# Reordering the first batch of an attention and mixer kernel: indices spread by a product, masks ahead of the data, casts on ScalarE

## The chip, the cores and the metric

The kernel runs on one core of a Trainium2 chip. The core has a matrix engine (TensorE, PE in the profile, with its weight loads as PEld), VectorE (DVE), ScalarE (ACT), GpSimd (POOL) and SyncE (SP), and 16 DMA engines that move data between memory and the core's SBUF. The engines run their own instruction lists in order and wait for each other by semaphores. The metric is the device time of one execution in microseconds, as the median of several runs.

## The reference

Eight batches with eight heads, 576 tokens and 64 elements a head. Attention is limited to a window of 32 tokens to either side, and eight tokens with given indices are global: they see all tokens, and all tokens see them. A token mixer and a channel mixer follow.

```python
scores = scale * np.matmul(q, k.transpose(0, 1, 3, 2))
mask = np.abs(pos[:, None] - pos[None, :]) <= window
mask = mask | is_global[:, None] | is_global[None, :]
attn = softmax(np.where(mask, scores, -1e9))        # written out in full
x = (attn @ v) with the heads side by side          # (8, 576, 512)
u = x + (np.maximum(x^T @ w_tok1, 0) @ w_tok2)^T
out = u + np.maximum(u @ w_ch1, 0) @ w_ch2
```

The indices are an input, so all masks that depend on them are made on the chip. The products run in float16, while inputs and the output are float32.

## The kernel before

The order of the instructions of each engine is the order in which the program is written: there is no planner, and an engine that waits holds back all that is written behind it. Two pools of PSUM tiles are used in turn: psS with three of them (scores, turned tiles, PV) and psM with two (the dense products).

A batch is worked on as follows. Heads are taken in four pairs p. `cast_qk` brings q and k to float16 (`qk`), and the last 64 of the 576 tokens of q and k together into `rn`. `T` turns a pair with products against an identity, `TE` copies the turned q and k from PSUM to `qT` and `kT`, including the last tokens. `S_` forms the scores of a pair in two parts and ACT takes the exponential into `e_all`. `SM` multiplies with the mask `bandm` on DVE. `GK` makes the rows of the global tokens (`lf`, masked by `mf`), `OG` their outputs (`rf`), and `PV` the product with v for each of five token tiles, with the division on DVE. `M1`, `M2` (for batch 0 `M23_first`) are the token mixer, `M3` turns its result, and `M4` and `M5` are the channel mixer, whose products are the list `dense`; `period(b)` spreads the dense products of batch b between the attention steps of batch b+1.

What comes ahead of `period(0)` is written out by hand at the end of the function (L781 to L860). There, the loads of q, k and v of batch 0 are issued from SP, pair by pair. Two loads from ACT's queue bring the indices: `gpp_i`, one index for each partition, and `gidx_b`, all eight for every partition (L78, L79). POOL writes constants and zero pads, makes `mf` in `masks_c` (L302, L303), clears the left part of `e_all` (L784), casts v in `castv`, issues the loads of the token mixer's weights (`load_wt`), the gathers of the global tokens' q and k of batches 0 to 3 (`gather(0)`, four indirect DMAs with the indices `idx_i`) and the loads of the channel mixer's first weights (`load_wc1`). Between the steps of the first pairs DVE makes the index masks: `masks_0` the one-hot tables for the global tokens of batch 0, `masks_a` the masks of rows and columns (with five products into `pcol`), `masks_b` their product with the band. `G0` picks the global tokens of batch 0 out of `qk` with a product. `gather_t(0)` stands between `PV(0,1)` and `PV(0,2)`: it casts what was gathered on ACT, turns it on PE and copies it.

In the first batch cast0(p) casts q on ACT and k on DVE. SP loads q and k of batch 1 into the same buffers as soon as these casts are done, ACT casts them after `GK(0)`, and `T(1,0)` and `T(1,1)` follow between the `PV` of batch 0.

Of the kernel before, what the change touches and what calls it, by code (L numbers as in the profile page):

```python
# [26 lines left out]
def kernel(  # L27
# [48 lines left out]
    gidx_b = const.tile([P, NG, 2], I32)  # L76
    gpp_i = const.tile([P, 1], I32)
    nc.scalar.dma_start(out=gpp_i, in_=bass.AP(tensor=gt32, offset=0, ap=[[0, P // NG], [2, NG], [1, 1]]))  # L78
    nc.scalar.dma_start(out=gidx_b.rearrange("p g w -> p (g w)"), in_=bass.AP(tensor=gt32, offset=0, ap=[[0, P], [1, 2 * NG]]))  # L79
# [32 lines left out]

    pi_i = const.tile([P, 1], I32)
# [26 lines left out]

    qk_pads(0)
# [30 lines left out]
    kgz = const.tile([P, B, NP, 2 * GW], F16)  # L172
    nc.vector.memset(kgz, 0.0)
    gpp = to_f("gpp", gpp_i, [P, 1])
    idx_i = const.tile([P, 4], I32)
    nc.vector.tensor_scalar(out=idx_i, in0=bc_f, scalar1=hb, scalar2=gpp, op0=ALU.add, op1=ALU.add)

    gpm = const.tile([P, 1], F32)
    nc.vector.tensor_scalar(out=gpm, in0=hi8, scalar1=-10000.0, scalar2=gpp, op0=ALU.mult, op1=ALU.add)
# [48 lines left out]
    e_all = const.tile([P, H, NT, EW], F16)  # L228
# [9 lines left out]

    def e_pads():
        nc.gpsimd.memset(e_all[:, :, 0, 64:P], 0.0)  # L240
        nc.gpsimd.memset(e_all[:, :, NT - 1, 64 + GW + P :], 0.0)

# [14 lines left out]

    def masks_0():
        nc.vector.tensor_copy(out=gidx_f, in_=gidx_b[:, :, 0])
        onehot(ohq, op_f, NT + 1)  # L260

    def masks_a():

        oht = const.tile([P, NT, NG], F32)
        isg = const.tile([P, NT], F32)
        onehot(oht, tp_f)
        nc.vector.reduce_sum(out=isg, in_=oht, axis=AX.X)
        isgb = const.tile([P, NT, P], F16)
        nc.vector.tensor_copy(out=isgb, in_=isg.unsqueeze(2).to_broadcast([P, NT, P]))
        pcol = [psm([P, 512], name="pcol0"), psm([P, P], name="pcol1")]  # L270
        for t in range(NT):
            nc.tensor.matmul(
                pcol[t // 4][:, P * (t % 4) : P * (t % 4) + P], lhsT=isgb[:, t, :], rhs=ident, start=True, stop=True
            )
# [9 lines left out]
        nc.vector.tensor_scalar(out=colng[:, 0:512], in0=pcol[0], scalar1=0.5, scalar2=None, op0=ALU.is_lt)  # L284
        nc.vector.tensor_scalar(out=colng[:, 512:S], in0=pcol[1][:, 0:LAST], scalar1=0.5, scalar2=None, op0=ALU.is_lt)
        nc.vector.memset(colng[:, S:], 0.0)

    def masks_b():
        rowh = const.tile([P, NT], F16)
        nc.vector.tensor_copy(out=rowh, in_=rowok)  # L290
        cn = colng.rearrange("p (c x) -> p c x", c=NT)
        bl, br = bandm[:, 1:NT, 0:64], bandm[:, :, 80:208]
        nc.vector.memset(bandm[:, 0, 0:64], 0.0)
        nc.vector.tensor_tensor(out=bl, in0=left.unsqueeze(1).to_broadcast([P, NT - 1, 64]), in1=cn[:, 0 : NT - 1, 64:P], op=ALU.mult)
        nc.vector.tensor_tensor(out=br, in0=right.unsqueeze(1).to_broadcast([P, NT, P]), in1=cn, op=ALU.mult)
        nc.vector.tensor_tensor(out=bl, in0=bl, in1=rowh[:, 1:NT].unsqueeze(2).to_broadcast([P, NT - 1, 64]), op=ALU.mult)
# [86 lines left out]
    def G0(p):  # L383

        if p == 0:
            st[0]["pg"] = psm([P, NP, 2, NG], name="pg0")
        pg = st[0]["pg"]
# [14 lines left out]
    def T(b, p):  # L402
        pT = pss([P, 2, 8 * P], F16, name=f"pT_{b}_{p}")
        for ti in range(2):
            for t in range(4):
                nc.tensor.transpose(out=pT[:, ti, P * t : P * t + P], in_=qk[:, ti, p, t], identity=ident)
        nc.tensor.transpose(out=pT[:, 1, 512:640], in_=rn[:, p], identity=ident)
        st[b]["pT", p] = pT

    def TE(b, p):  # L410
        pT = st[b]["pT", p]
        qT, kT = qTs[b % 2][:, p], kTs[b % 2][:, p]

        copy = nc.scalar.copy if b == 1 and p < 2 else nc.vector.tensor_copy
        pm = pT[:, 0, 0:512].rearrange("p (i t x) -> p t x i", i=4, t=4)
        copy(out=qT[:, 0:4, GW:QS].rearrange("p t (x i) -> p t x i", i=4), in_=pm)  # L416
        copy(out=qT[:, 4, GW : GW + LAST], in_=pT[:, 1, 512 : 512 + LAST])
        copy(  # L418
            out=kT[:, WIN : WIN + 512].rearrange("p (x i) -> p x i", i=4),
            in_=pT[:, 1, 0:512].rearrange("p (i x) -> p x i", i=4),  # L420
        )
        copy(out=kT[:, WIN + 512 : WIN + S], in_=pT[:, 1, 512 + LAST : 640])
# [168 lines left out]
    def M23_first(tau):  # L591
# [4 lines left out]
        for ch in range(2):  # L596
            nc.tensor.matmul(
                ps, lhsT=w2[:, ch, P * tau : P * tau + P], rhs=s["a1"][:, ch, :], start=(ch == 0), stop=(ch == 1)
            )
        nc.vector.tensor_add(out=s["u16"][:, tau], in0=x16s[0][:, tau], in1=ps)  # L600

    def M3_first(tau):
# [4 lines left out]
        nc.scalar.copy(out=s["uT"][:, :, P * tau : P * tau + P], in_=pu)  # L607
# [74 lines left out]
    def period(b):  # L682
# [12 lines left out]
        def scores(p, k):  # L695
# [12 lines left out]
            if n < 3 and p < 2:  # L708
                TE(n, p + 2)
# [53 lines left out]
        if n == 1:  # L763
            d(2)
            T(2, 0)
            TE(2, 0)
            T(2, 1)
            TE(2, 1)
# [7 lines left out]

    def cast0(p):
        cast_qk(0, 0, p, nc.scalar.copy)
        cast_qk(0, 1, p, nc.vector.tensor_copy)

    e_pads()  # L781
    pads(0)
    masks_c()
    nc.gpsimd.memset(e_all[:, :, :, 0:64], 0.0)  # L784
    castv(0)
    load_wt()
    gather(0)
    load_wc1(0)
    load_wc1(4)
    load_wc1(8)  # L790
    cast0(0)
    cast_qk(0, 0, None, nc.scalar.copy)
    masks_0()
    T(0, 0)
    cast0(1)
    TE(0, 0)
    G0(0)
    T(0, 1)
    cast0(2)
    TE(0, 1)  # L800
    es = S_(0, 0, 0)
# [91 lines left out]
```

## Time and profile before

| what | value |
|---|---|
| median of three runs | 329.54 us (328.32 to 329.64) |
| the profiled execution's own time | 328.06 us |
| its span | 326.0 us |
| busy PE, DVE, ACT, POOL | 296.4, 194.4, 163.8, 87.2 us |
| granted TensorE clock | 1.0 |

The span goes from the first to the last profiled instruction, and the profiled time has about two microseconds around it. A timeline row has the start, the length, the engine, the line, the operation, its output and inputs with their shapes, and in brackets how long the engine was idle before it and which work ended that. A row of groups has the number of instructions, their busy time together, the mean in ns of one, and the idle time ahead of them. The chain of work that ended last follows from the last instruction back to what released each. For a DMA, the profile gives the time from issue to landing.

### The profile page before, as it was taken

To read this page: it belongs to the slowest core of one execution; us is meant where nothing else is said; L and a number is where in the kernel's file an instruction comes from. 1 tells how busy PE (TensorE), PEld (TensorE's weight loads), DVE (VectorE), ACT (ScalarE), POOL (GpSimd) and SP (SyncE) were. 2 spreads that over 40 slices of the span, in tenths; PEclk is the share of its full clock that TensorE was granted. 3 is DMA by queue.
4 is the path that set the end of the run, shared out by engine and by line. 5 is a ranking of instruction groups with operands and counts; after the bars stand their busy time and mean duration, and the time that the engine had idled before them with its cause. 6 is when DMAs were issued, how large, how long until landed. Compare 5 with 4: busy or idle time off the path is not lost.

```text
span 326.0 us, 6430 instructions
## 1 busy us (share of the span) xinstructions
PE 296.4 (91%) x2541; PEld 155.6 (48%) x2541; DVE 194.4 (60%) x420; ACT 163.8 (50%) x296; POOL 87.2 (27%) x134
## 2 busy tenths in 40 slices
PE   1545989998999899999999999999999999999994
PEld 0333744544447444554457444644466445544641
DVE  4799558558774566767764557766773575360021
ACT  2439569411673846457645828385824455304600
POOL 8878957750593300230032000400000000000000
PEclk9999999999999999999999999999999999999999
DMA  5999999959379999794899289965530520043023
GB/s 137 267 263 165 203 178 272 180 155 275 103 180 214 153 223 318 112 90 110 262 234 114 50 238 294 124 66 144 125 56 13 148 68 2 0 87 125 0 72 92
DMA packets 107038, 48.18 MB, mean 148 GB/s; under 512 B 86336, under 2 KB 100544, under 8 KB 107008
## 3 DMA queue, kind: packets, MB, share of 16 engines
q1 hardware_dynamic: 67600, 32.52, 43.6%
q0 software_dynamic: 39120, 15.24, 38.8%
q8 instruction: 20, 0.33, 0.4%
q14 instruction: 10, 0.08, 0.1%
q10 hardware_dynamic: 288, 0.01, 0.0%
HBM read 36.12 MB, written 9.44 MB: 140 GB/s over the span
## 4 chain that ended last, share of the span: by engine, by line
PE 77%; DVE 13%; ACT 5%; DMA 2%; issue 1%; SPq 1%; DVEq 0%; ACTq 0%
PE op L653 28%; PE b1p L627 21%; PE a1p L556 5%; PE hp L580 4%; PE s L433 4%; PE b1lp L640 3%; DVE e_all L481 3%; PE pv L533 3%; PE pv L524 3%; PE pv L529 2%; ACT e_all L446 2%; DMA lk<-in_k_dram 2%; DVE qT L416 1%; ACT e_all L459 1%; ACT b L630 1%; DVE kT L418 1%
## 5 line engine op out<-in xcount | busy, mean ns | idle before, releaser
L627 PE MATMUL b1p<-uT,wc 128*128 128x512 f16 x384 | 94.8, 380 | 1.1 <-ACT b L630 0.3
L630 ACT ACTIVATE b<-b1p 128x512 f16<-128x512 f32 x96 | 58.4, 608 | 60.8 <-PE b1p L627 60.8
L653 PE MATMUL op<-wc,b 128*128 128x512 f16 x384 | 87.9, 379 | 0.0
L653 PEld LDWEIGHTS <-b 128*128 128x128 f16 x384 | 36.6, 98 | 43.8
L325 POOL DMA_DIRECT2D vsh<-in_v_dram x35 | 29.8, 867 | 96.4 <-PE pv L533 89.0
L627 PEld LDWEIGHTS <-wc 128*128 128x128 f16 x384 | 34.9, 98 | 43.3 <-issue 5.2
L446 ACT ACTIVATE e_all<-s 128x832 f16<-128x832 f32 x32 | 27.7, 866 | 52.9 <-issue 31.8
L657 DVE TENSOR_TENSOR osb<-u,op 128x512 f32<-128x512 f16 x32 | 22.0, 687 | 50.0 <-PE op L653 49.9
L481 DVE TENSOR_TENSOR e_all<-e_all,bandm 128x1040 f16<-128x1040 f16 x64 | 43.4, 718 | 1.2
L586 DVE TENSOR_TENSOR u<-x,hp 128x512 f16<-128x512 f16 x28 | 17.4, 683 | 21.6 <-PE hp L580 21.6
L541 DVE TENSOR_TENSOR x<-pv,rr 128x512 f16<-128x512 f32 (+1 forms) x40 | 27.6, 691 | 1.4
L524 PEld LDWEIGHTS <-e_all 128*128 128x128 f16 x320 | 22.0, 100 | 5.2 <-issue 0.2
L524 PE MATMUL pv<-vsh,e_all 128*128 128x66 f16 x320 | 24.3, 197 | 0.0
L433 PE MATMUL s<-qT,kT 64*128 64x208 f16 (+1 forms) x320 | 20.3, 254 | 4.2 <-DVE kT L418 1.8
L540 DVE RECIPROCAL rr<-pv 128x8 f32<-128x8 f32 (+1 forms) x40 | 8.3, 207 | 24.0 <-PE pv L533 23.8
L459 ACT ACTIVATE e_all<-s 128x576 f16<-128x576 f32 x32 | 20.9, 652 | 3.2 <-PE s L433 3.2
L529 PE MATMUL pv<-vsh,e_all 128*128 128x66 f16 x256 | 21.0, 198 | 0.0
L433 PEld LDWEIGHTS <-kT 64*128 64x128 f16 x320 | 12.0, 97 | 18.7 <-issue 12.6
L529 PEld LDWEIGHTS <-e_all 128*128 128x128 f16 x256 | 17.8, 101 | 3.4
L556 PE MATMUL a1p<-x,w 128*128 128x512 f16 x64 | 18.9, 379 | 0.0
L464 ACT ACTIVATE e_all<-s 128x416 f16<-128x416 f32 x32 | 17.1, 535 | 0.0
L533 PE MATMUL pv<-rf,lf 128*128 128x264 f16 x80 | 16.2, 285 | 0.9 <-DVE rf L508 0.9
(166 smaller groups left out, 343.5 us busy)
## 6 DMA issues: line engine op xcount, KB each, us to landing
out_dram<-osb SPq DMA_DIRECT2D x32, 256.0 KB, 3.2
lq<-in_q_dram SPq DMA_DIRECT2D x4, 1024.0 KB, 6.4
lk<-in_k_dram SPq DMA_DIRECT2D x4, 1024.0 KB, 8.9
wc<-in_moe_w_ch_dram POOLq DMA_DIRECT2D x6, 512.0 KB, 9.4
lq<-in_q_dram POOLq DMA_DIRECT2D x3, 1024.0 KB, 7.9
lk<-in_k_dram POOLq DMA_DIRECT2D x3, 1024.0 KB, 9.4
vsh<-in_v_dram POOLq DMA_DIRECT2D x21, 128.0 KB, 8.5
vsh<-in_v_dram POOLq DMA_DIRECT2D x14, 96.0 KB, 8.1
```

What stands on the lines that cost most here:

```text
L325: nc.gpsimd.dma_start(out=vsh[b % 2][r0:r1, c, :, 0:D], in_=v[b, :, j0 : j0 + (r1 - r0), :].rearrange("h p d -> p h d"),)
L433: nc.tensor.matmul(ps[:, par, off : off + n], lhsT=kT[r, P * c : P * c + P], rhs=qf[r, lo : lo + n], start=True, stop=True,)
L446: nc.scalar.activation(out=e2[:, :, 1:3, 64:EW], in_=ps[:, :, 0 : 2 * W].rearrange("p h (c x) -> p h c x", c=2), func=AF.Exp, scale=scale,)
L481: nc.vector.tensor_mul(out=eh, in0=eh, in1=bandm)
L524: nc.tensor.matmul(o, lhsT=e_all[:, h, tau, EW - P - sh : EW - sh], rhs=vsh[b % 2][:, tau, h, :], start=hh == 0, stop=False,)
L529: nc.tensor.matmul(o, lhsT=e_all[:, h, tau + 1, 0:P], rhs=vsh[b % 2][:, tau + 1, h, :], start=False, stop=False)
L533: nc.tensor.matmul(ps[:, hf, 0 : NP * VW], lhsT=s["lf"][:, P * tau - sh : P * tau - sh + P], rhs=s["rf"][:, 2 * hf : 2 * hf + 2], start=Fa ...
L541: nc.vector.tensor_tensor(out=x16s[b % 2][r, tau, :].rearrange("p (f h x) -> p f h x", f=2, h=NP), in0=pq[r, :, :, 0:D], in1=rr[r].unsquee ...
L556: nc.tensor.matmul(ps[tt], lhsT=w, rhs=x16s[b % 2][:, ch, :], start=(ch == 0), stop=(ch == NT - 1))
L627: nc.tensor.matmul(ps, lhsT=wc1[:, cc, P * j : P * j + P], rhs=s["uT"][:, cc, :], start=(cc == 0), stop=(cc == 3))
L630: nc.scalar.activation(out=s["b1"][:, j, :], in_=ps, func=AF.Relu)
L653: nc.tensor.matmul(ps, lhsT=w, rhs=wc2[:, j, :], start=(j == 0), stop=(j == NJ - 1))
```

## The change

The change is to the prologue, and to steps that the later batches share.

- The eight indices are loaded once, as one row in one partition (`gidx_1`), where two loads spread them over all partitions. `masks_0` casts the row and spreads it by a product with a row of ones into PSUM (`misc`). `positions()` works out `gpp`, `gpm` and `idx_i` on DVE from the spread indices and a selection table `sel`, and stands after the first scores.
- The zeros of `e_all` are written by DVE at the start, and no longer by POOL.
- `masks_0` and `masks_a` stand ahead of the casts of batch 0. The rest of the masks is split into `masks_b1`, `masks_b2` and `masks_b3`, which stand between the steps of the pairs.
- `cast0` puts q and k on ACT. In `TE` of the first two pairs q is copied by DVE and k by ACT, and the last tokens are turned for all four pairs in one step, `TR`, with two copies, in batches 0, 1 and 2.
- POOL's order becomes: pads, `load_wt`, `castv`, `masks_c`, `load_wc1(0)`, `gather(0)`, `load_wc1(4)`, `load_wc1(8)`.
- In `M23_first`, odd token tiles add x by a product with the identity and are copied by ACT; the last copy of `M3_first` is DVE's.
- `pcol`, `misc` and `pg` share two PSUM tiles that are taken once.

```diff
-    nc.scalar.dma_start(out=gpp_i, in_=bass.AP(tensor=gt32, offset=0, ap=[[0, P // NG], [2, NG], [1, 1]]))
-    nc.scalar.dma_start(out=gidx_b.rearrange("p g w -> p (g w)"), in_=bass.AP(tensor=gt32, offset=0, ap=[[0, P], [1, 2 * NG]]))
+    gidx_1 = const.tile([1, 2 * NG], I32)
+    nc.scalar.dma_start(out=gidx_1, in_=bass.AP(tensor=gt32, offset=0, ap=[[2 * NG, 1], [1, 2 * NG]]))
...
+    nc.vector.memset(ones, 1.0)
+    nc.vector.memset(e_all[:, :, :, 0:64], 0.0)
+    nc.vector.memset(e_all[:, :, 0, 64:P], 0.0)
+    nc.vector.memset(e_all[:, :, NT - 1, 64 + GW + P :], 0.0)
...
+    pm8 = int_op("pm8", 7, ALU.bitwise_and)
+    sel = to_f("sel", cc_i, [P, NG])
+    nc.vector.tensor_scalar(out=sel, in0=sel, scalar1=pm8, scalar2=None, op0=ALU.is_equal)
...
+    def positions():
+        nc.vector.tensor_mul(out=sel, in0=sel, in1=gidx_f)
+        nc.vector.reduce_sum(out=gpp, in_=sel, axis=AX.X)
+        nc.vector.tensor_scalar(out=gpm, in0=hi8, scalar1=-10000.0, scalar2=gpp, op0=ALU.mult, op1=ALU.add)
+        nc.vector.tensor_scalar(out=idx_i, in0=bc_f, scalar1=hb, scalar2=gpp, op0=ALU.add, op1=ALU.add)
...
     def masks_0():
-        nc.vector.tensor_copy(out=gidx_f, in_=gidx_b[:, :, 0])
+        gidx_h = const.tile([1, NG], F16)
+        nc.vector.tensor_copy(out=gidx_h, in_=gidx_1.rearrange("p (g w) -> p g w", w=2)[:, :, 0])
+        nc.tensor.matmul(misc[:, 0:NG], lhsT=ones, rhs=gidx_h, start=True, stop=True)
+        nc.vector.tensor_copy(out=gidx_f, in_=misc[:, 0:NG])
         onehot(ohq, op_f, NT + 1)
...
+    def TR(b, copy):
+        pr = pss([P, NP, P], F16, name=f"pr_{b}")
+        for p in range(NP):
+            nc.tensor.transpose(out=pr[:, p], in_=rn[:, p], identity=ident)
+        copy(out=qTs[b % 2][:, :, NT - 1, GW : GW + LAST], in_=pr[:, :, 0:LAST])
+        copy(out=kTs[b % 2][:, :, WIN + 512 : WIN + S], in_=pr[:, :, LAST:P])
...
+        if tau % 2 == 0:
+            nc.vector.tensor_add(out=s["u16"][:, tau], in0=x16s[0][:, tau], in1=ps)
+        else:
+            nc.tensor.matmul(ps, lhsT=ident, rhs=x16s[0][:, tau], start=False, stop=True)
+            nc.scalar.copy(out=s["u16"][:, tau], in_=ps)
...
+    qk_pads(0)
     pads(0)
-    masks_c()
-    nc.gpsimd.memset(e_all[:, :, :, 0:64], 0.0)
-    castv(0)
     load_wt()
+    castv(0)
+    nc.vector.memset(kgz, 0.0)
+    masks_0()
+    masks_a()
+    cast0(0)
+    T(0, 0)
+    cast_qk(0, 0, None, act)
+    TE_q(0, 0, dve)
+    TE_k(0, 0, act)
+    TR(0, dve)
+    G0(0)
+    cast0(1)
+    exps(S_(0, 0, 0))
+    T(0, 1)
+    positions()
+    masks_c()
+    load_wc1(0)
     gather(0)
-    load_wc1(0)
     load_wc1(4)
     load_wc1(8)
...
+    masks_b1()
+    TE_q(0, 1, dve)
     cast0(2)
+    exps(S_(0, 0, 1))
     G0(1)
+    TE_k(0, 1, act)
     T(0, 2)
+    masks_b2()
+    exps(S_(0, 1, 0))
+    TE(0, 2, dve)
     cast0(3)
+    exps(S_(0, 1, 1))
     G0(2)
     T(0, 3)
+    masks_b3()
+    exps(S_(0, 2, 0))
+    exps(S_(0, 2, 1))
+    SM(0, 0)
+    TE(0, 3, dve)
     G0(3)
     SM(0, 1)
+    exps(S_all(0, 3))
     GK(0)
+    SM(0, 2)
+    SM(0, 3)
     OG(0)
...
     gather_t(0)
+    TR(1, act)
```

125 lines of the change are left out of this document (47 added, 78 removed).

## The prediction

> **What bounds the kernel now.** I read the page first, then the chain in order of time, then the first 46 us engine by engine. The page gives the scale.
>
> ```profile
> span 326.0 us, 6430 instructions
> ...
> PE 296.4 (91%) x2541; PEld 155.6 (48%) x2541; DVE 194.4 (60%) x420; ACT 163.8 (50%) x296; POOL 87.2 (27%) x134
> ```
>
> PE bounds the whole, but not the start. The chain in order of time (start, length, what) is almost without a gap DVE's from 9.94 to the rf product, then goes over to PE, and from 46.12 on it is the b1p products of the regular periods.
>
> ```profile
> 9.94 0.57 DVE qk L336
> ...
> 31.57 0.72 DVE rf L508
> ...
> 46.12 0.97 PE b1p L627 x4
> ```
>
> So everything up to 46.1 us is prologue, and a microsecond won or lost there is carried to the end. The stretch from 9.94 to 32.28, by engine:
>
> ```profile
> 9.94:32.28 22.34, 12.44 (x146) 7.62 (x147) 21.43 (x58) 12.79 (x24) 18.47 (x23) 1.00 1.12 224
> ```
>
> The columns behind the length are busy PE, PEld, DVE, ACT, POOL, then PE clock, DMA share and GB/s. DVE is busy 21.43 of 22.34 us there; ACT has room; POOL has 18.47 us of work, which matters below.
>
> **The change, part by part.**
>
> DVE between 9.94 and 32.28 loses work. Its groups:
>
> ```profile
> L336 DVE CAST qk<-lk 128x512 f16<-128x512 f32 x3 | 3.6, 1210 | 2.3 <-DMA lk<-in_k_dram 2.3
> L418 DVE COPY kT<-pT 128x512 f16<-128x512 f16 x4 | 2.7, 678 | 0.0
> ...
> L481 DVE TENSOR_TENSOR e_all<-e_all,bandm 128x1040 f16<-128x1040 f16 x8 | 5.2, 696 | 0.2
> ...
> L422 DVE COPY kT<-pT 128x64 f16<-128x64 f16 x4 | 0.7, 178 | 0.0
> ...
> 17.72 0.19 DVE L253 TENSOR_TENSOR oht<-tp_f,gidx_f 128x40 f32<-128x40 f32 x1
> ...
> 20.03 0.68 DVE L284 TENSOR_SCALAR colng<-pcol 128x512 f16<-128x512 f32 x1
> ```
>
> A row of this view is count, busy us, mean ns, and idle time before; the last two rows are of the timeline (start, length). Gone: three k casts (3.6), two of four kT copies (1.36), and masks_a from 17.72 to 20.03 (2.3). The eight small last-token copies (L417 costs as L422, 1.4 together) become two larger ones, about 0.35 each by their size, between the 0.18 and 0.68 rows: saved 0.7. Added: positions(), four small operations of about 0.2 each, 0.8. Net 7.2 us less, so DVE has 14.2 us left. ACT, busy 12.79 us in this stretch, gets three casts at 0.62 (1.9) and two kT copies of about 0.68 (1.4): 16.1, so it has room, all the more as its casts of batch 1 are in the 12.79. Starting near 10, DVE could be done about 24.
>
> What is put ahead of the data costs nothing while the data is late. DVE does the e_all memsets first (3584 fp16 = 1792 words; by the kgz row below, 512 words, 3.5 times 0.48 = 1.7; by POOL's price of 2.22 for 2560 below, 3.1), then its old small operations (done by 2.85 now, when kgz starts), pm8 and sel and masks_0 (about nine small ones of 0.2, 1.8), kgz (0.48) and masks_a (2.3): 1.7 + 2.85 + 1.8 + 0.5 + 2.3 = 9.1. PE takes the pcol products and then the first transposes at about 9; the last tokens, cast at 8.60 now after 4.55 us of waiting, were not there much sooner. With POOL's price DVE would end at 10.5 and the front would start 1.4 later, which DVE's slack below swallows.
>
> ```profile
> 2.85 0.48 DVE L173 MEMSET kgz<- 128x512 uint32 x1
> 8.60 0.62 ACT L333 CAST rn<-lr 128x512 f16<-128x512 f32 x1 [4.55 <-DMA lr<-in_k_dram]
> 8.54 0.71 POOL L302 CAST it_f<-it_i 128x640 f32<-128x640 int32 x1
> 9.37 2.52 POOL L303 TENSOR_SCALAR mf<-it_f,gpm,hi 128x640 f16<-128x640 f32 x1
> 11.84 2.22 POOL L784 MEMSET e_all<- 128x2560 f16 x1
> 19.96 0.62 POOL L376 CAST vsh<-lv 96x512 f16<-96x512 f32 x1 [0.86 <-DMA lv<-in_v_dram]
> 20.99 0.98 POOL L203 DMA_DIRECT2D w<-in_moe_w_tok_dram  x1
> 24.20 1.06 POOL L189 DMA_INDIRECT g_q<-in_q_dram,idx_i  x1 [0.18 <-issue]
> 28.65 1.19 POOL L189 DMA_INDIRECT g_k<-in_k_dram,idx_i  x1 [0.31 <-issue]
> 29.84 2.37 POOL L210 DMA_DIRECT2D wc<-in_moe_w_ch_dram  x3
> ```
>
> POOL is what sets the end. These rows, in time, show its queue. The second k cast on DVE fell beside the memset at 11.84: three such casts took 3.6 us where the chain's first took 0.57, so some 1.9 us of DVE time go with that memset too. [...]
>
> New POOL order: the pads, load_wt, castv, then masks_c, load_wc1(0), gather(0). load_wt is issued at about 8 instead of 20.99, while q, k and v of batch 0 are still coming. That is a second transfer against the first. The DMA at its steady rate and in the stretch with w alone:
>
> ```profile
> 9.00:10.00 1.00, 0.68 (x13) 0.60 (x14) 0.06 (x1) 0.80 (x2) 0.89 (x2) 1.00 1.10 348
> 26.00:27.00 1.00, 0.94 (x12) 0.24 (x8) 0.96 (x4) 1.00 (x3) 0.88 (x1) 1.00 1.46 197
> 5.00:6.00 1.00, 0.00 (x0) 0.00 (x0) 0.00 (x0) 0.00 (x0) 1.00 (x4) 1.00 0.32 67
> w<-in_moe_w_tok_dram POOLq DMA_DIRECT2D x1, 288.0 KB, 7.2
> w<-in_moe_w_tok_dram POOLq DMA_DIRECT2D x1, 256.0 KB, 7.4
> w1l<-in_moe_w_tok_dram POOLq DMA_DIRECT2D x2, 32.0 KB, 6.4
> ```
>
> The w loads are 608 KB at 200 GB/s: 3.1 us of full DMA. Everything behind them (v, then batch 1's q and k) moves back by that if they share; bounds 0 (they wait for the other queue) and 3.6 (1.25 MB of float32 at 348). Against it: from 5 to 6 us the DMA is used to 0.32 while the two broadcast index loads are still landing; with one row instead they are gone. The tail of k, lr, took 5.9 us to land from its issue at 2.6 and 4.3 from 154.6, in a later batch with nothing on ACT's queue (the first two rows below; the third is the last gather of the first half), so I take about 1.4 us of head start for all that follows, between 0 and 1.9.
>
> ```profile
> DMA to landing us min/median/max: 5.9/5.9/5.9
> DMA to landing us min/median/max: 4.3/4.3/4.3
> DMA to landing us min/median/max: 2.8/2.8/2.8
> 33.26 0.35 ACT L309 CAST g_k<-g_k 128x128 f16<-128x128 f32 x1
> 34.25 0.26 PE L524 MATMUL pv<-vsh,e_all 128*128 128x66 f16 x1
> ```
>
> The sum on that path: last v landed 19.96 − 1.4 + 3.1 = 21.7; cast 0.62: 22.3; masks_c, 8.54 to 11.89 now, 3.35: 25.6; one wc1 issue 0.8: 26.4; from first to last gather issue 24.20 to 28.65, 4.45: 30.9; landing 2.8 (third row): 33.7. gather_t on ACT casts (0.35), PE transposes and only then takes PV(0,2), about 0.65 later: 34.35, against 34.25 now. mf is ready at 25.6, lf follows on DVE (0.5), then two SM (twice 0.70 and an eg of 0.2 each, 1.6) and rf 0.72: 30.1 instead of 32.28. So PV(0,0) and PV(0,1) come 2 us earlier and then PE waits, because gather_t stands ahead of PV(0,2) in program order. Other way round, the second batch's k lands at 26 − 1.4 + 3.1 = 27.7, and the seven casts behind it at 0.62 end at 32.0, inside the gather. The DVE gain is real and goes into a new wait. Plus 0.1 us.
>
> M23_first: odd taus lose a DVE add and get a product and an ACT copy.
>
> ```profile
> 43.26 1.34 DVE L600 TENSOR_TENSOR u<-x,hp 128x512 f16<-128x512 f16 x2 [0.33 <-PE hp L597]
> 44.44 1.24 ACT L607 COPY uT<-pu 128x512 f16<-128x512 f16 x2 [0.37 <-PE pu L606]
> ```
>
> ACT now does u1, uT0, uT1, u3, uT2 in line at 0.62; uT3 on DVE ends near 45.9 where ACT ends at 45.68 now: plus 0.25 (bounds −0.6, one add saved, and +0.6, one copy more).
>
> TR(2) in period 1 stands where this copy is on the chain, and frees rn for the POOL cast that waits 15.68 us for the last transposes.
>
> ```profile
> 78.27 0.60 DVE qT L416
> 85.43 0.65 POOL L333 CAST rn<-lr 128x512 f16<-128x512 f32 x1 [15.68 <-PE pT L407]
> ```
>
> Two copies of 0.35 come ahead of the first scores of batch 2 instead of two of 0.18, and 0.36 goes from each of the three later turns: between +0.4 and −0.7. The POOL casts of batch 3 start up to 7 us sooner, beside DVE work on the chain, where the conflict above may cost as much as it saves later. POOL's loads after the gathers move by about a microsecond. I take all of it at 0 with ±0.5: its cover is PE, 91% busy.
>
> Sum: +0.1 + 0.25 + 0.0 = about +0.35 on this execution's 328.06 us (span 326.0 and 2.06 around it): 328.4. The three runs have the median 329.54, 1.48 above it; there the sum is 329.9.
>
> **The rivals.**
>
> Faster: w yields. The w loads wait until SP's queue is empty, as they may do now: 288 KB took 7.2 us to land from 20.99, though 512 KB of wc1 from 29.84 took 5.5.
>
> ```profile
> DMA to landing us min/median/max: 5.5/5.5/5.5
> ```
>
> Then v is not delayed: castv ends at 19.96 − 1.4 + 0.62 = 19.2, the last gather is issued at 27.8, but stands behind w (24.6 to 27.7) and wc1(0) (2.6 more, 512 KB at 200): 30.7. PV(0,2) at 31.35, −2.9, with M23 −2.65: 326.9. Against it: the lateness alone shows no strict order. DMA was full until 26 (the row 26 to 27 is the first under 200 GB/s), and equal shares would have made w late as well. [...] The trace has no clear overlap of two such loads.
>
> Slower: no head start. If the index loads did not slow the data (0 instead of 1.4) and w costs its 3.6, castv ends at 24.2, the gathers land at 35.6 and PV(0,2) starts at 36.25: +2.0, with M23 +2.25: 331.8. It decides from a castv end of 23.6, where the total passes +1.65. For it: DMA is full well before 10 us and until 26, and nothing after the gather can make up for it, since PE is busy 12.38 of the 13.77 us to 46.05.
>
> ```profile
> 32.28:46.05 13.77, 12.38 (x132) 7.95 (x131) 8.43 (x17) 7.72 (x21) 10.77 (x19) 1.00 1.50 187
> ```
>
> DVE stays the bound is a third: with 14.2 us of work it ends before POOL in any of these cases, so I give it 0.02 and count it with the first.
>
> **How the numbers follow.** Two runs of one kernel differ by up to 0.4% here, so 0.5%, 1.65 us, is taken as what can be told from no change. Forecast (gather takes back what DVE gives): 0.41, with its own range 328.3 to 331.2. w yields: 0.33. No head start: 0.26. The forecast's tails give a little to each side: faster 0.34, same 0.39, slower 0.27. The range from 326.4 to 332.6 takes in both rivals and the ±0.5 of the later parts; outside it I leave 2 in 10. The predicted time is the forecast's, 329.9.
>
> **What would show it.** DVE from 10 us on with some 14 us of work and one wait of 2 us or more at lf (L495's multiply) for POOL's mf; POOL's last v cast at 22.3; the last gather issue at 30.9 and a wait of ACT's g_k cast for it; PE idle ahead of PV(0,2), which starts near 34.35; b1p first near 46.3. It is wrong if v lands at 18.6 (w yields), if the last v cast starts after 23 (no head start), if wc1(0) ahead of the gathers holds them back for longer than its issue, or if the time from PV(0,2) to the first b1p is not the 11.8 us of now.

## The result

The changed kernel takes 327.17 us (median of 20 runs, 325.7 to 329.07) and the kernel before 329.69 (20 runs, 328.32 to 332.28): ratio 0.9922, 95% interval 0.9902 to 0.9942. The forecast was 329.9, that is no change; the time lies inside the range from 326.4 to 332.6. The profiled execution took 327.19 us, near the median; the one of before took 328.06, faster than any of its 20 timed runs. So the two traces are only 0.9 us apart where the medians are 2.5 apart, and part of the question is where the other 1.6 us are.

The page of the changed kernel, then its chain in order of time (start, length, what):

```profile
span 325.3 us, 6421 instructions
...
PE 296.6 (91%) x2544; PEld 156.6 (48%) x2544; DVE 191.3 (59%) x407; ACT 167.3 (51%) x301; POOL 83.2 (26%) x131
```

```profile
18.99 2.31 DVE e_all L497 x2
...
28.91 1.20 POOL g_k L196
...
46.09 0.97 PE b1p L649 x4
```

In this view DVE no longer holds the chain up to the rf product: it hands over to POOL's gathers. That part of the chain is not the path, though. It reaches the first hp product by a load of wc that POOL issues at 34.59 and that lands at 42.5, after that product has begun (40.91). What the product reads is ScalarE's a, which ends at 40.86. The b1p products of the regular periods begin at the same moment as before (46.02 against 46.05). The two stretches by engine, columns as in the prediction:

```profile
9.94:32.28 22.34, 13.31 (x172) 8.76 (x171) 18.17 (x43) 17.12 (x33) 16.27 (x21) 1.00 0.98 219
32.28:46.05 13.77, 12.27 (x118) 7.53 (x116) 6.60 (x14) 6.90 (x16) 11.33 (x18) 1.00 1.52 176
```

DVE has 4.2 us of idle time in the first stretch, where it had 0.9. POOL's queue, then ACT's cast of the last gather, DVE's rf, the turns of what was gathered and of `rn`, x of PV(0,1), and the first product of PV(0,2), from the changed kernel's timeline (start, length, and in brackets what ended the idle time before):

```profile
12.27 1.92 POOL L386 CAST vsh<-lv 32x512 f16<-32x512 f32 x3 [1.50 <-DMA lv<-in_v_dram]
17.07 0.64 POOL L386 CAST vsh<-lv 128x512 f16<-128x512 f32 x1 [2.88 <-DMA lv<-in_v_dram]
17.97 1.50 POOL L386 CAST vsh<-lv 128x512 f16<-128x512 f32 x2 [0.25 <-DMA lv<-in_v_dram]
20.24 3.36 POOL L313 TENSOR_SCALAR mf<-it_f,gpm,hi 128x640 f16<-128x640 f32 x1
24.70 1.08 POOL L196 DMA_INDIRECT g_q<-in_q_dram,idx_i  x1 [0.30 <-DVE e_all L497]
28.91 1.20 POOL L196 DMA_INDIRECT g_k<-in_k_dram,idx_i  x1 [0.30 <-issue]
31.51 0.30 ACT L319 CAST g_k<-g_k 128x128 f16<-128x128 f32 x1 [0.97 <-DMA g_k<-in_k_dram,idx_i]
29.61 0.71 DVE L524 TENSOR_TENSOR rf<-og,blk 128x528 f16<-128x528 f32 x1 [0.32 <-PE og L519]
32.20 0.31 PE L320 MATMUL pg<-ident,g_k 128*128 128x128 f16 x1
32.30 0.63 PE L436 MATMUL pr<-ident,rn 128*128 128x128 f16 x4
32.57 0.69 DVE L557 TENSOR_TENSOR x<-pv,rr 128x512 f16<-128x512 f32 x1
33.32 0.24 PE L540 MATMUL pv<-vsh,e_all 128*128 128x66 f16 x1 [0.39 <-DVE x L557]
```

The last v cast ends at 19.5 instead of 20.6, although the token weights are now loaded in front of it; rf starts 1.96 us earlier (31.57 before), PV(0,2) only 0.93 (34.25 before), b1p 0.03. Each step hands on less than it got.

The gather delays ACT's cast by 0.97 us, but not PV(0,2). TensorE starts the last products of PV(0,0) at 30.38, right behind rf, and has no gap up to the end of the turns at 32.93; the turn of g_k at 32.20 finds its cast done (31.81). Then it waits 0.39 us for DVE's x of PV(0,1): `TR(1)` takes a PSUM tile of its own ahead of PV(0,2), so that PV(0,2) gets the tile of PV(0,1). The turns of `TR(1)` and this wait are about 1 us, and the kernel before has neither.

The last loss is in TensorE's pace. The eight turns of T(1,0) and T(1,1) and the token products beside them, in the trace of the changed kernel:

```profile
34.62 1.06 PE L414 MATMUL pT<-ident,qk 128*128 128x128 f16 x8
35.47 1.06 PE L572 MATMUL a1p<-x,w 128*128 128x512 f16 x2
...
37.32 0.61 PE L414 MATMUL pT<-ident,qk 128*128 128x128 f16 x8
37.77 0.59 PE L572 MATMUL a1p<-x,w 128*128 128x512 f16 x2
```

The same work takes 1.06 us and then 0.61. TensorE runs at about half pace until 36.95 us, and in the profiled execution of before only to 35.69. These are the starts of the first clock records of the two traces, and the durations of equal products change there. Ahead of its first record a trace has no clock, and the clock column of the profile says 1.00: in this stretch it can't be read, the durations can.

### The profile page after: what moved, and what is told of

The parts are those of the page before. It is cut to its first block, busy times and chain, and to the rows that moved or that the text cites. A ratio compares the mean times of both kernels' runs of the same rounds, so it can differ in the third digit from the quotient of the medians.

```text
span 325.3 us, 6421 instructions
## 1 busy us (share of the span) xinstructions
PE 296.6 (91%) x2544; PEld 156.6 (48%) x2544; DVE 191.3 (59%) x407; ACT 167.3 (51%) x301; POOL 83.2 (26%) x131
## 4 chain that ended last, share of the span: by engine, by line
PE 77%; DVE 9%; ACT 6%; POOL 3%; DMA 2%; issue 1%; ACTq 0%; DVEq 0%
PE op L675 28%; PE b1p L649 21%; PE a1p L572 5%; PE s L449 4%; PE hp L596 4%; PE b1lp L662 3%; PE pv L540 3%; PE pv L549 2%; ACT e_all L462 2%; PE pv L545 2%; DMA wc<-in_moe_w_ch_dram 2%; DVE e_all L497 2%; ACT e_all L475 1%; ACT b L652 1%; DVE qT L418 1%
## 5 line engine op out<-in xcount | busy, mean ns | idle before, releaser
L540 PEld LDWEIGHTS <-e_all 128*128 128x128 f16 x320 | 22.2, 101 | 6.0 <-DVE x L557 0.7
L596 PE MATMUL hp<-a,w 128*128 128x512 f16 x72 | 16.8, 378 | 0.0
```

The source lines that it names most:

```text
L540: nc.tensor.matmul(o, lhsT=e_all[:, h, tau, EW - P - sh : EW - sh], rhs=vsh[b % 2][:, tau, h, :], start=hh == 0, stop=False,)
L596: nc.tensor.matmul(ps[:, i, :], lhsT=w2[:, ch, P * tau - sh : P * tau - sh + P], rhs=s["a1"][:, ch, :], start=(ch == 0), stop=(ch == 1),)
```

## The experiments

Times are medians; ratios are to the kernel before on the same chip, whose medians were 328.62, 328.71, 329.32 and 328.56 in the four comparisons. The places from the traces, in us. "Full pace" is the start of the last clock record at the full clock, which in all of them lasts into the last 3 us of the span:

```
kernel                 rf     g_k cast  PV(0,2)  b1p    PV to b1p  b1p, batch 2   full pace
before                 31.57  33.26     34.25    46.05  11.80      125.01         35.69
before_again           31.66  33.35     34.35    46.31  11.96      125.19         36.11
after                  29.61  31.51     33.32    46.02  12.70      124.28         36.95
after_again            29.31  31.70     33.01    44.12  11.11      122.08         33.27
before_1row            30.57  31.99     33.26    45.53  12.27      124.13         35.70
before_1row_tr         30.52  32.22     33.21    45.72  12.51      123.96         36.11
after_bcast            29.87  33.90     34.76    47.01  12.25      125.05         37.41
after_turn_late        28.32  31.90     32.76    44.84  12.08      123.95         35.07
after_w_late           29.10  34.78     35.63    48.84  13.21      127.03         40.31
after_warm             31.39  32.46     34.70    46.23  11.53      124.25         35.89
before_warm            32.11  33.72     34.28    45.56  11.28      124.83         31.85
after_warm2            29.21  31.46     32.60    43.60  11.00      122.59         22.17
after_warm3            29.27  31.70     32.65    43.65  11.00      122.29         23.65
before_warm2           33.15  33.11     36.09    47.22  11.13      125.82         32.47
before_1row_tr_warm    31.78  31.79     34.72    45.85  11.13      123.93         31.06
warm2_gather_first     29.10  31.86     32.49    43.49  11.00      121.46         21.03
warm2_w_late           28.42  30.68     31.80    42.80  11.00      122.77         20.71
best                   30.02  32.36     32.83    44.15  11.32      123.10         23.29
```

The traced execution is not always near the median: those of after_bcast (327.77 us) and after_again (324.99) are the fastest of theirs, 2.0 and 1.7 us below the medians.

### The index row, alone and taken back

The theory was that two loads broadcast to 128 partitions slow all that is loaded beside them. One kernel puts the row into the kernel before, the other puts the broadcast loads back into the changed one.

```
before_1row, in the kernel before:
- nc.scalar.dma_start(out=gpp_i, ...); nc.scalar.dma_start(out=gidx_b..., ap=[[0, P], [1, 2 * NG]])
+ nc.scalar.dma_start(out=gidx_1, ... ap=[[2 * NG, 1], [1, 2 * NG]])
+ gidx_h = gidx_1's low words as f16; matmul(pg0[:, 128:128 + NG], lhsT=ones, rhs=gidx_h); gidx_f = copy
after_bcast, in the changed kernel: the reverse
```

> The kernel before with the indices as one row spread by a product (gidx_1, sel and the small operations for gpp ahead of the data on DVE), and nothing else of the change. Theory: the two broadcast loads hold up the first q and k by 2 us, and in most executions by more than in the profiled one; without them the data is earlier, DVE starts its 22 us of work about 1.5 us sooner, and the time falls by 1.2 to 2 us against the kernel before. Rival: DVE has the same work and the data's earlier landing is worth under 0.5 us.

> The changed kernel with the two broadcast loads of the indices back in place of the one row and its product. Theory: these two loads hold up q, k and v by 2 to 2.5 us (q and k of the first pair landed at 4.4 instead of 6.5), so v, the gather and ACT's g_k cast come about 2 us later, and the time is 1.5 to 2 us over the changed kernel's, near 328.9. Rival: the early weights are what sets v, the index loads do not matter, 327.2 +- 0.5.

The row alone: 327.05 us (326.64 to 327.27), 0.9944 (0.9927 to 0.9961). The whole change without it: 329.78 (327.77 to 330.44), 1.003 (1.0014 to 1.0045). So the rest of the change is not faster without the row. In the trace TR(2) still saves its 0.8 us there (next part), but PV(0,2) starts at 34.76, later than in the kernel before (34.25). The DMA view of the first 32 us shows why, first for the changed kernel and then with the broadcast loads back (GB/s in slices of 0.8 us, the ACT queue's packets, and how long k took to land):

```profile
GB/s 0 0 87 335 281 203 263 296 305 320 348 337 318 276 239 201 202 195 212 275 294 192 189 220 220 262 383 324 364 381 362 289 165 206 196 181 49 0 41 23
...
q10 hardware_dynamic: 2, 0.00, 0.0%
...
lk<-in_k_dram SPq DMA_DIRECT2D x4, 256.0 KB, 3.9
```

```profile
GB/s 0 0 36 275 127 209 19 65 276 310 342 350 347 346 328 207 194 186 195 198 213 268 284 193 237 146 214 158 347 367 344 316 357 379 326 201 212 204 129 63
...
q10 hardware_dynamic: 288, 0.01, 0.5%
...
lk<-in_k_dram SPq DMA_DIRECT2D x4, 256.0 KB, 5.9
...
gidx_b<-in_global_idx_dram ACTq DMA_DIRECT2D x1, 8.0 KB, 5.8
```

From 3.2 to 6.4 us the four slices move 127, 209, 19 and 65 GB/s instead of 281, 203, 263 and 296. With 288 packets that hold 0.01 MB in all, the 256 KB loads of k take 2.0 us longer to land (medians of four). Neither their bytes nor their own time is that much: 0.5% of the 16 engines' 32 us is some 0.16 us on each engine, an estimate from the view. What the other packets wait for is not shown, nor whether the number of packets, their size or their spread over the partitions matters.

The delay grows along SP's queue, as the later loads are also issued later. The last load of v is issued at 14.07 and lands at 19.91 in the kernel before, and at 12.08 and 15.93 in before_1row: 4.0 us sooner. In the changed kernel it lands at 18.80, and at 21.00 with the broadcast loads: 2.2 us. The prediction took 1.4 for all loads.

### TR(2)

```
after_turn_late, in the changed kernel, for batch 2 only:
- TR(2, nc.vector.tensor_copy) ahead of T(2, 0)
+ one turn of rn[:, p] and two small copies in each T(2, p), TE(2, p)
before_1row_tr: before_1row with the reverse
```

> The changed kernel with TR undone for batch 2 alone: its last tokens are turned pair by pair, as before. Theory: TR(2) frees rn, so POOL's casts of batch 3 run from 77.6 instead of 85.4 and no longer beside the second e_all multiply of DVE (1.31 us instead of 2.01), which is worth 0.7 us; the time is 0.7 us over the changed kernel's and the casts start at about 85 again. Rival: these 0.7 us come from the prologue, and nothing changes here.

> The kernel before with two parts of the change alone: the indices as one row, spread by a product, and the last tokens of batch 2 turned together (TR(2)). If these two are the whole gain, they add up: 0.9944 for the one row and 0.6 us (0.0018) for TR(2) make a ratio of 0.9925 with some 0.001 to either side, where the whole change gives 0.992 to 0.994. If the casts on ScalarE, the masks put ahead and the new order of POOL bring something of their own, this kernel stays behind the changed one by 0.5 us or more (ratio above 0.995); if they cost something, it is ahead of it (ratio below 0.991). In period 1 the e_all multiply beside the casts of batch 3 takes 1.3 us instead of 2.0, and the step from the first product of batch 1 to that of batch 2 falls from 41.2 to about 40.5 us.

Without TR(2) the changed kernel takes 327.27 us (326.25 to 328.09), 0.9957 (0.9941 to 0.9973), where a new execution of the changed kernel took 326.67 beside it; from b1p of batch 1 to that of batch 2 it needs 41.18 us instead of 40.42. With the row and TR(2) alone the kernel before comes to 327.05 (326.56 to 327.39), 0.9937 (0.9917 to 0.9956), and to 40.42. The times alone would not settle it, since the two intervals overlap. The step does: it is 41.18 to 41.20 in every trace without TR(2), and 40.42 or 40.43 in every trace with it but one (41.17 in warm2_w_late, see below). The multiplies of scores and mask around 87 us in period 1, before and after:

```profile
86.92 0.37 DVE L475 TENSOR_TENSOR eg<-e_all,bandm 128x160 f16<-128x160 f16 x1
87.32 2.01 DVE L481 TENSOR_TENSOR e_all<-e_all,bandm 128x1040 f16<-128x1040 f16 x2
```

```profile
86.77 0.23 DVE L491 TENSOR_TENSOR eg<-e_all,bandm 128x160 f16<-128x160 f16 x1
87.03 1.31 DVE L497 TENSOR_TENSOR e_all<-e_all,bandm 128x1040 f16<-128x1040 f16 x2
```

POOL's casts of batch 3, which start at 77.63 now and started at 85.43, no longer lie beside them. Row and TR(2) together give what the whole change gives (0.9937 here, 0.9922 and 0.9937 in the two comparisons of the changed kernel). The masks put ahead, the casts on ScalarE and POOL's new order add nothing that these runs can tell, and an effect under about 1 us would not be seen in the times. The traces show where it goes: these parts bring rf from 30.5 to 29.3 and 29.6, but PV(0,2) starts at 33.21 and 33.26 with the row and without them, and at 33.01 and 33.32 in the two executions of the changed kernel.

### The token weights behind the gather

```
- pads(0); load_wt(); castv(0)
+ pads(0); castv(0)
...
- gather(0); load_wc1(4)
+ gather(0); load_wt(); load_wc1(4)
```

> The changed kernel with one thing put back: load_wt() (the loads of the token weights w1 and w2) is called behind gather(0) instead of ahead of castv(0). If the early weight loads delay v through shared transfers, the last v chunk lands at 16 to 17 us (18.8 with them early, 15.9 in the run of the one-row indices alone), castv ends at 16.5 to 17.5 instead of 19.4, the gathers end at about 26 instead of 28.9, and ACT's g_k cast runs at 28.5 to 29.5 instead of 31.5. If the gather is what sets the front's end, the time falls by 0.5 to 2 us, ratio to the kernel before 0.988 to 0.992. If the scores and DVE are close behind (rf at 29.6 as in the changed kernel), or the lead is lost in a stretch with TensorE at half pace, g_k comes 2 to 3 us sooner and the time stays, ratio 0.992 to 0.994. If the weights, now landing later, are what the first token product waits for (behind 33 us), the time rises, ratio above 0.995.

329.92 us (329.11 to 331.8), 1.002 (1.0001 to 1.0039): slower than the changed kernel by about 1%. None of the three expectations names the reason. The first half came as predicted: castv ends at 16.9 and the last gather is issued at 25.43. But then ACT waits, in the trace of this kernel:

```profile
30.94 0.62 ACT L346 CAST qk<-lk 128x512 f16<-128x512 f32 x1 [4.44 <-DMA lk<-in_k_dram]
...
34.78 0.29 ACT L319 CAST g_k<-g_k 128x128 f16<-128x128 f32 x1
```

The casts of batch 1 stand ahead of gather_t(0) on ACT, and batch 1's k, 1 MB, now lands at 30.9 instead of 26.6. It is issued 1.0 us later, wc1(0) and the gathers are issued 3.4 us sooner, and w comes behind them, so that all of them are loaded beside it; the run does not split them. So the early w loads do put v back (POOL waits up to 2.88 us for a part of it above and 0.45 here), and with them in front batch 1's k takes 8.4 us to land instead of 11.8. The second effect is the larger: PV(0,2) comes 2.3 us later than in the changed kernel's first trace.

### TensorE's pace

before_again and after_again are the two kernels unchanged, in other executions. The others add products that nobody reads, meant to bring TensorE to full pace sooner and to keep it there. That more work does this was the author's estimate; full pace begins at 22.17 us in after_warm2, and at 36.95 and 33.27 in the two traces of the changed kernel.

```
fill(n): n times nc.tensor.matmul(<unused columns of a PSUM tile>, lhsT=ident, rhs=ident)
after_warm:           fill(25) ahead of S_all(0, 3), 18 + 10 in OG(0); columns of misc
after_warm2, _warm3:  fill(25), 28 + 18 in OG(0), 3 x 9 about PV(0, 0) and PV(0, 1); columns of pcol
before_warm:          fill(28) behind TE(0, 2), 9 + 11 in OG(0)
before_warm2:         fill(28), 30 inside masks_a, 28 + 18, 3 x 9
before_1row_tr_warm:  the same with 40 for 28, in before_1row_tr
```

> The kernel before, unchanged, for a second profile. Its profiled execution was at 328.06 us, below the median of its runs, 329.69. If its executions differ in the prologue, the first b1p product starts later than 46.05 here by about as much as the time is over 328.06; if they differ later, it starts at 46.0 +- 0.2 again and a later period is longer.

> The changed kernel, unchanged, beside the others on one chip. On the first chip it was 0.9922 of the kernel before; 0.992 +- 0.003 is expected, with the first b1p product near 46.0 and the second period 0.7 us shorter than before in the profile.

The kernel before took 328.23 us (one execution) with b1p at 46.31. The changed kernel took 326.67 (324.99 to 327.44), 0.9937 (0.9915 to 0.9959), and its trace differs from the first one mainly in one thing:

```profile
33.83 0.61 PE L414 MATMUL pT<-ident,qk 128*128 128x128 f16 x8
34.28 0.59 PE L572 MATMUL a1p<-x,w 128*128 128x512 f16 x2
```

T(1,0) runs at full pace here and b1p comes at 44.12, 1.9 us sooner: 0.3 us lie ahead of PV(0,2), and 1.6 between it and b1p (11.11 instead of 12.70), with the same instructions. The change of pace lies near 33.3 us in one execution and near 37.0 in the other, 3.7 us apart. The clock records that begin and end inside a kernel last 3.41 (after_warm), 6.83 (before_warm2, before_1row_tr_warm) or 10.24 us (before_warm): one, two or three times 3.41. What sets the moment of the change in an execution is not shown.

All 18 traces of the table follow one rule. PV(0,2) to b1p takes 10.9 to 11.3 us, plus half of the time from PV(0,2) to the full pace where that comes later: 11.80 in before is 11.08 and half of 1.44, 12.70 in after is 10.89 and half of 3.63, 13.21 in after_w_late is 10.87 and half of 4.68. So the pair of profiles hides 1.1 us of what the change gives: before was traced with 1.44 us of half pace behind PV(0,2), the changed kernel with 3.63. With the 0.9 us that the two traces are apart, the change is worth about 2.0 us at equal pace, an estimate from these rows and close to the 2.0 and 2.5 us of the medians.

> The changed kernel with 53 unused 128-column products against the identity in three waits of PE (25 ahead of the scores of pair 3, 18 and 10 in OG), written to columns nobody reads. Theory: the lead of the changed prologue (rf 2 us earlier) is lost because PE's products run at half pace until 36.9 us (a turn of eight takes 1.06 us at 34.62 and 0.61 at 37.32). With PE kept at work the full pace comes before 33, the first b1p product starts at 44.6 instead of 46.02, and the time falls by 1.4 us to about 325.8. Rival: the gather and the turn of the PSUM tiles hold PE there whatever its pace; the first b1p stays at 46.0 and the time at 327.2.

> The kernel before with 48 such unused products (28 ahead of the pcol products, 9 and 11 in OG). Theory of the pace: full pace comes some 3 us sooner than 36.0, the first b1p product starts about 0.9 us sooner, near 45.1, the time falls to about 328.8, and its runs, from 328.3 to 332.3 us now, spread less. Rival: DVE sets the prologue, so that nothing changes (329.7).

after_warm took 327.15 us (326.56 to 328.62), 0.9956 (0.994 to 0.9971), and leaves the question open: its products waited for a reader of their tile, held the scores of pair 3 back (rf at 31.39), and the pace fell again at 32.5. before_warm took 327.94 (327.3 to 328.69), 0.9971 (0.9959 to 0.9984), with b1p 0.5 us earlier.

> The changed kernel with 98 unused products, now written to the first pcol tile, which has no open reader there (in after_warm they waited for a reader of misc and held the scores of pair 3 back by 2 us, and PE fell back to half pace at 32.5): 25 ahead of the scores of pair 3, 28 and 18 in OG, 9 ahead of the last products of PV(0,0) and PV(0,1) each, 9 ahead of gather_t. Theory of the pace: PE is at full pace from some point between 22 and 29 us on, PV(0,2) to the first b1p takes 11.5 us instead of 12.7, b1p starts at 44.8 +- 0.5, and the time is 1.2 us below the changed kernel's. Rival: b1p at 46.0 and the time as the changed kernel's.

> The changed kernel with its 98 filler products once more, for the same chip as the two kernels beside it: first b1 product at 43.6 us, ratio 0.9906 as in the first comparison, within 0.002.

Full pace from 22.2 and 23.7 us on: 325.67 us (325.22 to 326.56), 0.9906 (0.9887 to 0.9925), and on another chip 325.38 (325.18 to 326.39), 0.9917 (0.9903 to 0.9931). PV(0,2) to b1p is 11.00 us both times, and the times spread over 1.3 and 1.2 us (6 and 5 executions) instead of 2.5 and 3.4 (6 and 20). About 1 us of the changed kernel's time is this pace (326.67 and 325.67 on one chip; the intervals overlap).

> The kernel before with filler products (extra work whose result nobody reads: 28 behind the second batch of turns, 30 between the column masks' products, 46 in OG(0), 27 around PV(0,0) and PV(0,1)), so that TensorE comes to full pace at about 18 us and keeps it. If the pace were the whole difference of the two kernels, this one would come to the time of the changed kernel with its fillers (0.9906 in its own comparison). If the change has a lead of its own, PV(0,2) stays near 34 us, the first b1 product comes at 45 to 45.6 us instead of 43.6, and the ratio is 0.995 to 0.998: some 0.6% behind the changed kernel with fillers, of which 0.2% is TR(2).

> The kernel before with the one-row indices, TR(2) and filler products (as in the kernel before with fillers, 40 instead of 28 at the first place; their result is not read). If these two parts are the whole gain, it is level with the changed kernel and its fillers: first b1 product within 0.5 us of 43.6, the ratio within 0.001 of it. If the masks put ahead, the casts on ScalarE and POOL's order bring something that half pace hid (rf at 30.5 here, 29.2 there), it is 0.6 to 1.3 us slower, ratio 0.993 to 0.995. If those parts cost something, it is faster.

328.54 us (327.99 to 329.3), 1.000 (0.999 to 1.001), and 326.08 (325.71 to 326.76), 0.9928 (0.9915 to 0.994). They don't show how much the two kernels differ at equal pace: in both the pace fell back to half just where OG(0) stands. The stretches of before_warm2:

```profile
24.00:26.00 2.00, 0.99 (x20) 0.75 (x17) 1.85 (x9) 1.75 (x4) 1.39 (x3) 0.91 1.28 274
...
28.00:30.00 2.00, 2.00 (x22) 2.00 (x20) 1.97 (x5) 2.00 (x6) 2.00 (x3) 0.50 0.35 82
...
32.00:34.00 2.00, 2.00 (x50) 1.79 (x49) 0.71 (x1) 1.46 (x5) 1.89 (x6) 0.88 1.21 199
```

The clock, which the trace does record here, drops near 25.6 us and comes back near 32.5. TensorE has only 0.99 us of work in the two us from 24, the pace falls, and then 46 fillers at half pace stand in front of the last products of OG(0): rf 1.6 us later than without them. In the 3.41 us (the shortest record) ahead of each of the four falls inside the prologue TensorE is busy for 1.1 to 2.0 us. That too little work makes the pace fall fits this, but it is not shown: before_1row_tr_warm keeps the pace through 13.99 to 17.40 us with 1.71 us of work. Only the pace after PV(0,2) is equal, and there the kernels agree (11.13 and 11.00).

### Beyond both kernels

```
warm2_gather_first: after_warm2 with gather(0) ahead of load_wc1(0)
warm2_w_late:       after_warm2 with gather(0), load_wt(), load_wc1(0) in this order behind masks_c()
best:               warm2_w_late with TR(1) moved from ahead of PV(0, 2) to behind M1(0, 1)
```

> The changed kernel with its fillers, and gather(0) ahead of load_wc1(0) on POOL. If the gather holds PV(0,2), the four gathers start 0.8 us sooner and land with fewer bytes beside them: g_k cast 0.5 to 1.5 us before the 31.5 us of the kernel with fillers alone, PV(0,2) and the time 0.3 to 1 us less. If ScalarE's casts of batch 1 (which wait for their k) or PV(0,0)'s x on DVE are as late, the cast moves up and PV(0,2) does not: equal to 0.3 us. If load_wc1(0), 1.1 us or more later, is now late for the first b1 product, it is slower.

> The changed kernel with the 98 filler products (extra work whose result nobody reads) and with the token weights loaded behind gather(0), which itself is ahead of load_wc1(0). TensorE is at full pace from about 22 us here, so nothing of a head start in front of PV(0,2) can be lost in a stretch at half pace. If the gather sets the front's end, g_k is cast at 28 to 29 us instead of 31.5, and the first b1 product comes 0.7 to 2 us sooner than the 43.6 us with the fillers alone: 41.6 to 42.9, the time 323.8 to 325.0. If the scores on ScalarE and DVE are the next bound right behind it, the first b1 product stays within 0.5 us of 43.6 and the time within 0.4 of 325.67.

> As the kernel with fillers and late token weights, and TR(1) moved from ahead of PV(0,2) to behind PV(0,3), so that its tile pr no longer takes the psS turn in front of PV(0,2) and PV(0,2) no longer waits for PV(0,0)'s x on DVE. If that turn is a cost on the path, PV(0,2) starts 0.3 to 1 us sooner against the other kernel and the time falls by as much; if ScalarE's copies of batch 1 then come too late for the scores of period 0, the first b1 product is as early and the time to that of batch 1 grows by up to 0.5 us; if the gather or the scores hold PV(0,2) anyway, the two kernels are equal to 0.3 us. In any case the time should be at or below that of the fillers alone, 325.7.

325.14 us (324.7 to 326.14), 0.9906 (0.9891 to 0.9921); 326.78 (325.14 to 328.86), 0.9931 (0.9909 to 0.9953); 326.29 (325.64 to 327.19), 0.9916 (0.9895 to 0.9937). None is apart from after_warm2 by more than the intervals. The first has the lowest median of the case, 0.9% below the kernel before, but not below the changed kernel with its fillers by more than the runs can tell (325.38 on the same chip), and its g_k cast did not come sooner (31.86). It no longer waits for the gather; ACT is still at the casts of batch 1, since their k makes it wait 1.52 us (0.51 in after_warm2):

```profile
28.02 0.62 ACT L346 CAST qk<-lk 128x512 f16<-128x512 f32 x1 [1.52 <-DMA lk<-in_k_dram]
...
31.86 0.29 ACT L319 CAST g_k<-g_k 128x128 f16<-128x128 f32 x1
```

In warm2_w_late the first b1p comes at 42.80, as the first expectation has it, and the time does not follow: b1p of batch 2 is at 122.77, later than in after_warm2 and after_warm3. POOL's casts of batch 3, now from 75.2 us on, meet DVE's multiplies again (up to 1.10 us for one, 0.69 alone), the step from batch 1 to batch 2 is 41.17 us instead of 40.42, and the one before it 38.80 instead of 38.57 and 38.21. In best the wait between g_k's cast and PV(0,2) shrinks from 1.14 us (after_warm2) to 0.47, so TR(1) in front of PV(0,2) did cost (by the turn of the three tiles PV(0,2) waits for x of PV(0,1), not of PV(0,0) as the expectation has it); but g_k's cast is 0.9 us later there, because batch 1's k is, and the gain is gone. Gather, batch 1's k and the psS turn lie within a microsecond of each other.

## Why the prediction was wrong

- **The prologue carries to the end:** right from batch 1 on. From b1p of batch 2 on all traces keep their distance to before to 0.12 us, and all but one to 0.07. In period 0 it is not: from the first b1p to that of batch 1 the traces take 37.4 to 38.8 us, so up to a microsecond of a lead is lost or won there (after_warm2 38.57, after_again 37.55).
- **DVE loses 7.2 us:** 4.0 (21.43 to 32.28 before; 17.46 us of work from 9.74 to the end of rf at 30.32 now). colng (1.0) stayed in the stretch, and POOL's castv and longer masks_c now lie beside DVE's bandm, eg and e_all, which take 1.2, 1.4 and 6.2 us instead of 0.8, 0.9 and 5.2. That DVE's gain would go into waits was right; it waits for ScalarE's lf (1.29) and not, as written, for mf.

```profile
9.74:30.32 20.58, 11.61 (x152) 7.34 (x151) 17.46 (x41) 16.60 (x32) 14.52 (x17) 1.00 1.04 239
```

- **What is put ahead of the data is free:** right, masks_a ended at 9.15 (9.1 forecast). That rf ended at 30.32 (30.1) is luck: the forecast has it wait for mf until 25.6, but mf is ready at 23.60, and 3.3 us more of DVE work than forecast and the wait for lf take its place.
- **Head start 1.4 us, between 0 and 1.9:** this term failed. It was read from the tail of k, lr (5.9 us to land, 4.3 in a later batch), and used for all that follows. k and lr do land 2.0 us sooner (lr of k at 6.54 instead of 8.51), but the sum goes by the last load of v. With the row and with w behind the gather that lands at 16.25 (after_w_late) instead of 19.91: 3.7 us. Some of it is the execution: in before_again v lands at 18.49.
- **w in front of v costs 3.1:** 2.55, from 16.25 to 18.80. The sum had v land at 21.7. What was not counted is batch 1's k, which takes 8.4 us to land with w in front and 11.8 with w behind the gather: that gives back more than w costs.
- **POOL sets the front's end:** this path failed with it. With v at 18.80, castv ends at 19.5 (22.3 forecast) and the gathers land at 31.5 (33.7). g_k's cast still waits 0.97 us for them, but TensorE takes what was gathered 0.4 us after it is cast. PV(0,2) starts at 33.32 (34.35), set by rf, by the turns of TR(1) and by x of PV(0,1); the prediction did not look for the PSUM turn that TR(1)'s tile takes. In after_bcast and after_w_late TensorE does wait for ACT's g_q cast at this place (1.51 and 3.2 us); ACT is late there with batch 1's casts.
- **PV(0,2) to b1p stays 11.8 us:** wrong, as its own condition says. It is 12.70 and 11.11 in two executions of the changed kernel, by where the change of pace falls, and 11.00 at full pace throughout. The 11.80 in the profile of before was one case of this.
- **M23_first +0.25:** 0. From the a1 copy to b1p it takes 5.76 us (40.26 to 46.02) and took 5.78.
- **TR(2) at 0, between +0.4 and −0.7:** this term failed too: −0.77 in the step from batch 1 to batch 2 of the profiled pair (40.43 after 41.20), 0.6 in the times without it. The earlier POOL casts were seen, and their conflict with DVE taken to cost as much as it saves; they fall into a stretch with no long DVE multiply, and the pair around 87 us takes 1.31 us instead of 2.01.

Neither rival came true: w does not yield (v lands at 18.80 with it in front and at 16.25 with it behind), so "w yields" had nearly the right time (326.9) for a wrong reason, and there is a head start. The third, that DVE stays the bound, was given 0.02 and is nearer: it is rf, the end of DVE's work, that TensorE follows to PV(0,2).

So the forecast of no change failed at two terms, the head start of v (3.7 instead of 1.4), which took the gather off the path, and TR(2) (−0.77 instead of 0). The row and TR(2) make up the gain of the medians: 1.66 us for the row in its own comparison and 0.6 for TR(2). Together 2.3, and the medians differ by 2.5 us in the first comparison and by 2.0 in the second. What stays open is in how many executions of either kernel the pace changes early, and so how much of it is in these medians: the runs meant for equal pace lost it.

## What to carry to other kernels

A load that is broadcast from DRAM to all partitions can cost far more than its bytes (here two of them, 0.01 MB in 288 packets, cost the 256 KB loads of k 2.0 us, medians of four): read the queue's packet count, and if it is large against its bytes, try one row that is spread by a product. Read a head start at the load that the sum goes by, not at the first one. Check the chain of a profile against the rows: whether the release that it names comes before what it is said to release. When transfers are reordered, ask of each load both what it delays and what it is no longer beside; and before a lead of a microsecond in front of TensorE is counted, look at the durations of equal products (here 1.06 and 0.61 us for eight turns) to see at which pace the work behind it runs, and compare several executions.

## What the runs showed of the hardware

- Two loads of 288 packets with 0.01 MB in all on ACT's queue delay the 256 KB loads of k on SP's queue by 2.0 us (3.9 to 5.9 us to land, medians of four) and the last load of v by 2.2 us (18.80 to 21.00, after and after_bcast) to 4.0 us (15.93 to 19.91, before_1row and before).
- The change from half to full pace moved by some 3.7 us between two executions of one kernel (33.27 and 36.95), worth 1.6 us (11.11 and 12.70 from PV(0,2) to b1p): each microsecond of half pace behind PV(0,2) cost half a microsecond in the 18 traces. The pace was lost again in before_warm2, from 25.6 to 32.5 us.
- A pair of DVE's multiplies of two fp16 tensors, 128x1040, took 2.01 us with POOL's casts of batch 3 beside it (before, from 87.32 on) and 1.31 without them (after, from 87.03 on); with castv's last casts and masks_c beside it (after, from 18.99 on, POOL at 17.97 to 23.60) a pair took 2.31.
